# Splitting every large load between the SP and the ACT queue in a decode attention and gated MLP kernel

## The chip, the core and the metric

The kernel runs on one NeuronCore of a Trainium2 chip. TensorE (PE) does the matmuls and transposes, VectorE (DVE) and ScalarE (ACT) the elementwise work, GpSimd (POOL) builds a few masks, and SyncE (SP) issues transfers. A transfer is spread over the core's 16 DMA engines. The metric is the device time of one execution in microseconds (us): 198.85 us, median of 3 runs (198.69 to 199.15).

## The reference

Two blocks work on the same four token vectors, and a sigmoid gate mixes them:

```
g = sigmoid((x * gate_w).sum(-1))                       # x: 4 tokens x 512
q = x @ wq                                              # 32 heads of 128
k, v = last 4096 positions of the caches, 8 kv heads    # 4 batches
a = softmax(q k^T / sqrt(128)) v  @ wo
b = (relu(x @ W_gate) * (x @ W_up)) @ W_down            # 512 -> 1792 -> 512
return g * a + (1 - g) * b
```

All tensors are bf16. Keys and values of the window are 32 MB each, `wq` and `wo` 4 MB each, and the three MLP weights 1.75 MB each. Nothing that is read is used for more than four tokens, so 81 MB come in for little arithmetic.

## The kernel before

The work is cut into eight sets (`NSET`): one batch and four of its kv heads each, that is one 4 MB load of K and one of V (`load_k`, L157, `load_v`, L161). Each of the 128 partitions takes 16,384 columns (32 KB) of a load. `Ksb` and `Vsb` have two buffers each, used in turn. `Wbig` holds `wq` first and `wo` later; the MLP weights go into the K and V buffers when sets 6 and 7 leave them free (L172 to L178).

A small class, `Program`, keeps a list of instructions for each engine, in the order in which the code adds them. `P.op` adds an instruction and `P.dma` a transfer, each with a name that others may wait for. A transfer has its own semaphore, which is complete at 16. The waits stand in front of the instruction on its engine, so whatever an engine has in its list behind a waiting instruction waits too. All large loads are issued by SP, which has nothing else to do: `WQ`, `K0`, `K1`, `V0`, `K2`, `V1` and so on to `K7`, `V6`, then `WG`, `WU` (gate and up), `V7`, `WD` (down) and four pieces `WO 0..3` of `wo` (16, 10, 4 and 2 of its 32 rows of 512 columns, `WO_CUTS`). `K s` waits for the last scores of set s-2, event `("SC", s-2, 3)`; `V s` for the last values matmul of set s-2, `("PV", s-2, 3)`. ACT issues two small loads at the start, `X` (4 KB) and `GW` (1 KB).

One stage s runs the scores of set s beside the softmax and the values of set s-1. The order on each engine is written out by hand (L403 to L432). In a stage PE transposes K in 16 fills of four 128x128 blocks (`kt`, L261), ACT and DVE copy them back over K (L266 for the nine fills in `ACT_TAKES`, L268 for the rest), PE forms scores in four banks (L282), DVE adds a mask and takes maxima (L290), ACT takes exponents in two pieces (L319), DVE transposes them (L326), and PE multiplies with V (`values`, L338). `combine` (L351 to L361) sums the partial results of a set and scales them. The end of a stage on PE is: values piece 1, fill 15, values piece 2, scores bank 3 (which gives `SC s 3`), values piece 3 (which gives `PV s-1 3`). After it DVE finds the maximum (`maximum`, L294) and PE starts fill 0 of the next stage, which waits for `K s+1`; the first copy after it, of fill 0, is ACT's.

After stage 7 come the last exponents, `combine(6)`, the gate and up matmuls (`gateup`, L386), the last values, `combine(7)`, the down matmuls (L446) and the `wo` matmuls (L454), which take the four pieces in order, then one copy (L458) and the store (L459).

Of the kernel before, what the change touches and what calls it, by code (L numbers as in the profile page):

```python
# [13 lines left out]
HQ = 32  # L14
# [5 lines left out]
NSET = 8  # L20
# [59 lines left out]
def bass_gated_mix__sliding_block_cached__glu_gated_reglu__decode_kernel(  # L80
# [13 lines left out]
    with ExitStack() as ctx:  # L94
# [58 lines left out]
        def heads(cache, s):  # L153
            b, half = s // 2, s % 2
            return cache[b, 4 * half:4 * half + 4, SK - WIN:SK, :].rearrange("h (r c) d -> r h (c d)", r=32)

        def load_k(s):  # L157
            P.dma("sp", lambda e: e.dma_start(Ksb[:, s % 2, :], heads(A_k_cache, s)), ("K", s),
                  [("SC", s - 2, NBANK - 1)] if s >= 2 else [])

        def load_v(s):  # L161
            P.dma("sp", lambda e: e.dma_start(Vsb[:, s % 2, :], heads(A_v_cache, s)), ("V", s),
                  [("PV", s - 2, 3)] if s >= 2 else [])

        P.dma("act", lambda e: e.dma_start(xsb[0:4, :], A_x.rearrange("b o d -> (b o) d")), ("X",))
        P.dma("act", lambda e: e.dma_start(xsb[4:5, :], gate_w.rearrange("(o d) -> o d", o=1)), ("GW",))
        P.dma("sp", lambda e: e.dma_start(Wbig[:, :], A_wq.rearrange("(p t) w -> p (t w)", p=128)), ("WQ",))  # L167
        load_k(0)
        for s in range(1, NSET):
            load_k(s)  # L170
            load_v(s - 1)
        P.dma("sp", lambda e: e.dma_start(Ksb[:, 0, 0:4 * FF], B_W_gate.rearrange("(p t) f -> p (t f)", p=128)),  # L172
              ("WG",), [("SC", NSET - 2, NBANK - 1)])
        P.dma("sp", lambda e: e.dma_start(Ksb[:, 0, 4 * FF:8 * FF], B_W_up.rearrange("(p t) f -> p (t f)", p=128)),
              ("WU",), [("SC", NSET - 2, NBANK - 1)])
        load_v(NSET - 1)
        P.dma("sp", lambda e: e.dma_start(Vsb[:, 0, 0:NFT * 512], B_W_down.rearrange("(p i) w -> p (i w)", p=128)),  # L177
              ("WD",), [("PV", NSET - 2, 3)])  # L178
        wo_src = A_wo.rearrange("(p i) w -> p (i w)", p=128)
        for k in range(len(WO_CUTS) - 1):  # L180
            lo, hi = 512 * WO_CUTS[k], 512 * WO_CUTS[k + 1]
            P.dma("sp", lambda e, lo=lo, hi=hi: e.dma_start(Wbig[:, lo:hi], wo_src[:, lo:hi]), ("WO", k), [("Q",)])  # L182


        P.op("pool", lambda e: e.memset(ones[:, :], 1.0), ("ONES",))
# [64 lines left out]
        def kt(s, i):  # L250
            f = len(fills)
            fills.append((s, i))
            tr_of[(s, i)] = f
            bk = trb(f)
            kw = Ksb[:, s % 2, :].bitcast(FP32)
            for cc in range(4):
                c = 4 * i + cc
                w = []
                if cc == 0:
                    w = [("K", s), ("IDENTF",)] + ([copy_done(f - NTR)] if f >= NTR else [])  # L260
                P.op("pe", lambda e, bk=bk, cc=cc, c=c, s=s: e.transpose(  # L261
                    bk[:, cc * 128:(cc + 1) * 128], kw[:, c * 128:(c + 1) * 128], identf[:, :]),
                    ("KT", s, i) if cc == 3 else None, w)
            dst = Ksb[:, s % 2, i * 1024:(i + 1) * 1024]
            if i in ACT_TAKES:
                P.op("act", lambda e: e.activation(dst, bk[:, :].bitcast(BF16), ACTF.Copy), ("KTC", s, i), [("KT", s, i)])  # L266
            else:
                P.op("dve", lambda e: e.tensor_copy(dst, bk[:, :].bitcast(BF16)), ("KTC", s, i), [("KT", s, i)])  # L268
# [60 lines left out]
        def values(s, k):  # L329
            par = s % 2  # L330
            v3 = Vsb[:, par, :].rearrange("p (c w) -> p c w", w=256)
            for c in range(16):
                g = c % 4
                w = []
                if c == 0:
                    w = [("PTT", s, k * NPIECE // 4), ("V", s), ("OSB", s - 1) if s >= 1 else None]
                col = (16 * k + c) * 32
                P.op("pe", lambda e, c=c, g=g, col=col: e.matmul(  # L338
                    OB[32 * g:32 * g + 32, 0:256], pT[:, par, col:col + 32], v3[:, 16 * k + c, :],
                    start=(k == 0 and c < 4), stop=(k == 3 and c >= 12), tile_position=(0, 32 * g)),  # L340
                    ("PV", s, k) if c == 15 else None, w)
            if k == 3:
                P.op("dve", lambda e: e.tensor_copy(osb[:, par, :], OB[:, 0:256]), ("OSB", s),  # L343
                     [("PV", s, 3), ("SUMS", s - 2) if s >= 2 else None])
# [18 lines left out]
        def qproj():  # L363
            for h in range(HQ):
                for t in range(4):
                    P.op("pe", lambda e, h=h, t=t: e.matmul(  # L366
                        FB[:, 64 + 4 * h:68 + 4 * h], Wq3[:, t, 128 * h:128 * h + 128], xT[:, t * 8:t * 8 + 4],
                        start=(t == 0), stop=(t == 3)),
                        ("Q",) if (h == HQ - 1 and t == 3) else None, [("WQ",), ("XTC",), ("G",)])
            P.op("dve", lambda e: e.tensor_copy(qTb[:, :].rearrange("p (b h) -> p b h", b=4),  # L370
                                                FB[:, 64:192].rearrange("p (h b) -> p b h", b=4)), ("QB",), [("Q",)])
            for h in range(2):
                P.op("pe", lambda e, h=h: e.matmul(OB[:, 128 * h:128 * h + 128], perm[:, h, :], qTb[:, :], start=True, stop=True),
                     ("QP",) if h == 1 else None, [("QB",), ("PERM", 1)])
            for g in range(2):
                r = slice(64 * g, 64 * g + 64)
                P.op("dve", lambda e, g=g, r=r: e.tensor_copy(
                    QS[r, :, 16 * g:16 * g + 16], OB[r, 0:256].rearrange("p (s j) -> p s j", j=16)),
                    ("QC", g), [("QP",), ("QZ",)])

        def gateup():
            for i in range(NFT):
                for which, W, key in ((0, Wg, "WG"), (1, Wu, "WU")):
                    col = 64 + 64 * which + 4 * i
                    for t in range(4):
                        P.op("pe", lambda e, W=W, i=i, t=t, col=col: e.matmul(  # L386
                            FB[:, col:col + 4], W[:, t, i:i + NFT * 127 + 1:NFT], xT[:, t * 8:t * 8 + 4],
                            start=(t == 0), stop=(t == 3)),
                            ("GU",) if (i == NFT - 1 and which == 1 and t == 3) else None, [("WG",), ("WU",), ("OQ", NSET - 2)])
            P.op("dve", lambda e: e.tensor_scalar(gtmp[:, :], FB[:, 64:64 + NFT * 4], 0.0, None, op0=ALU.max), ("H0",), [("GU",)])  # L390
            P.op("dve", lambda e: e.tensor_tensor(gtmp2[:, :], FB[:, 128:128 + NFT * 4], gtmp[:, :], ALU.mult), ("H1",), [("H0",)])
            P.op("dve", lambda e: e.tensor_tensor(  # L392
                hT[:, :, :].rearrange("p i (b o) -> p i b o", o=8)[:, :, :, 0], gtmp2[:, :].rearrange("p (i b) -> p i b", b=4),
                gsb[:, 4:8].rearrange("p (o b) -> p o b", o=1).to_broadcast([128, NFT, 4]), ALU.mult), ("H",),
                [("H1",), ("G",), ("HZ",)])
# [4 lines left out]
            kt(0, i)  # L400
        for m in range(NBANK):
            scores(0, m)
        for s in range(1, NSET):  # L403
            maximum(s - 1)
            kt(s, 0)
# [24 lines left out]
            values(s - 1, 2)  # L430
            scores(s, 3)
            values(s - 1, 3)  # L432
        maximum(NSET - 1)
        for k in range(NPIECE):
            exponent(NSET - 1, k)
# [8 lines left out]
        for i in range(NFT):  # L444
            for cb in range(4):
                P.op("pe", lambda e, i=i, cb=cb: e.matmul(  # L446
                    AB[32 * cb:32 * cb + 32, 0:128], hT[:, i, :], Wd[:, i, cb * 128:(cb + 1) * 128],
                    start=(i == 0), stop=False, tile_position=(0, 32 * cb)), None,
                    [("WD",), ("H",), ("SCC", NSET - 1, NBANK - 1)])
        for k in range(len(WO_CUTS) - 1):  # L450
            for i in range(WO_CUTS[k], WO_CUTS[k + 1]):
                for cb in range(4):
                    last = i == 31 and cb == 3
                    P.op("pe", lambda e, i=i, cb=cb: e.matmul(  # L454
                        AB[32 * cb:32 * cb + 32, 0:128], oq[:, i, :], Wo3[:, i, cb * 128:(cb + 1) * 128],
                        start=False, stop=(i == 31), tile_position=(0, 32 * cb)),
                        ("ACC",) if last else None, [("WO", k), ("OQ", NSET - 1)])
        P.op("dve", lambda e: e.tensor_copy(outs[:, :], AB[:, 0:128]), ("OUTS",), [("ACC",)])  # L458
        P.dma("sp", lambda e: e.dma_start(out.rearrange("b o (c d) -> c (b o) d", d=128), outs[0:128:8, :]), ("OUT",), [("OUTS",)])  # L459
        P.op("sp", None, None, [("OUT",)])  # L460
# [50 lines left out]
```

## Time and profile before

| | |
|---|---|
| Time, median of 3 runs | 198.85 us |
| The profiled execution's own time | 198.96 us |
| Its span | 197.1 us |
| Bytes moved | 81.27 MB, 412 GB/s over the span |
| PE, DVE, ACT busy | 71%, 52%, 46% of the span |
| K loads, issue to landing (median) | 23.3 us |
| V loads, issue to landing (median) | 32.4 us |
| Last `wo` piece, issue to landing | 23.8 us |

The span is the time from the first to the last record of the profiled execution; 1.9 us of its time lie outside it. The profile page also cuts the span in 40 slices and gives for each the busy share of every engine and of the 16 DMA engines. The chain that ended last follows the last instruction back through what released each step. The trace also keeps a record of every DMA packet (its queue, start, length and bytes); a packet here is one partition's run of a load, 32 KB for a K or V load.

### The profile page before, as it was taken

What the parts mean: (1) busy time and instruction counts of PE and PEld (TensorE: products, weight loads), DVE (VectorE), ACT (ScalarE), POOL (GpSimd) and SP (SyncE); (2) the same over time, 40 slices, a digit from 0 to 9 for tenths busy, and PEclk for the clock granted to TensorE, in tenths of its full rate; (3) what the DMA queues carried; (4) which work ended last, traced back from release to release, by engine and by line L of the source; (5) the groups of instructions that cost most, each with busy time, mean ns of one, the idle gap of its engine ahead of it and who ended that gap; (6) DMA issues with size and microseconds to landing.
All of it is one profiled execution on the core that took longest, in us unless ns stands there. A gap on an engine that the chain in (4) does not pass through costs nothing.

```text
span 197.1 us, 4202 instructions
## 1 busy us (share of the span) xinstructions
PE 140.5 (71%) x1858; PEld 107.1 (54%) x1858; DVE 103.4 (52%) x278; ACT 91.6 (46%) x108; POOL 6.1 (3%) x31
## 2 busy tenths in 40 slices
PE   0134099869789829994998399839991999497734
PEld 0033087536466428753865386438751875397533
DVE  2102044998589446855694388437845595741200
ACT  2000069698298309760983288319740876220000
POOL 7400000000000000000000000000000000000000
PEclk9999999999999975998899979966997599965855
DMA  6999999999999999999999999999999999999980
GB/s 220 426 445 452 435 445 439 422 426 421 429 426 426 422 426 432 424 439 429 445 432 435 432 426 417 432 439 429 432 426 422 432 399 425 449 435 406 421 340 32
DMA packets 3503, 81.27 MB, mean 412 GB/s; under 512 B 409, under 2 KB 414, under 8 KB 670
## 3 DMA queue, kind: packets, MB, share of 16 engines
q1 hardware_dynamic: 3476, 81.01, 96.2%
q8 instruction: 14, 0.23, 0.5%
q14 instruction: 3, 0.02, 0.0%
q10 hardware_dynamic: 10, 0.01, 0.0%
HBM read 81.01 MB, written 0.00 MB: 411 GB/s over the span
## 4 chain that ended last, share of the span: by engine, by line
DMA 58%; PE 29%; ACT 9%; DVE 2%; issue 1%; SPq 1%
DMA Ksb<-in_A_k_cache_dram 46%; PE bank L261 18%; DMA Wbig<-in_A_wo_dram 12%; ACT Ksb L266 7%; PE bank L282 5%; PE bank L338 2%; PE bank L351 2%; DVE Ksb L268 1%; ACT sc L319 1%; PE bank L454 1%; ACT L319 1%; SPq L182 0%; SPq L167 0%; SPq L177 0%; DVE outs L458 0%
## 5 line engine op out<-in xcount | busy, mean ns | idle before, releaser
L261 PE MATMUL bank<-identf,Ksb 128*128 128x128 f32 x512 | 81.0, 312 | 31.0 <-DMA Ksb<-in_A_k_cache_dram 26.5
L266 ACT ACTIVATE Ksb<-bank 128x1024 bf16<-128x1024 bf16 x72 | 70.9, 1022 | 69.2 <-PE bank L261 68.8
L261 PEld LDWEIGHTS bank<-identf,Ksb 128*128 128x128 f32 x512 | 66.1, 160 | 46.0 <-DMA Ksb<-in_A_k_cache_dram 28.4
L268 DVE COPY Ksb<-bank 128x1024 bf16<-128x1024 bf16 x56 | 38.0, 685 | 43.0 <-PE bank L261 42.0
L290 DVE CUSTOM_DVE_ANT_0 sc<-bank,mask 128x512 bf16<-128x512 f32 x32 | 21.7, 684 | 9.5 <-PE bank L282 9.4
L338 PE MATMUL bank<-Vsb,pT 128*32 128x256 bf16 x512 | 20.8, 291 | 1.0 <-DVE hT L392 1.0
L282 PE MATMUL bank<-Ksb,QS 128*32 128x512 bf16 x256 | 19.4, 384 | 2.1 <-DVE Ksb L268 1.6
L326 DVE STREAM_TRANSPOSE pT<-sc 128x1024 bf16<-128x1024 bf16 x16 | 19.7, 1236 | 1.7 <-ACT sc L319 1.5
L319 ACT ACTIVATE sc<-sc,negmax 128x1024 bf16<-128x1024 bf16 x16 | 18.3, 1146 | 4.8 <-DVE negmax L311 4.7
L338 PEld LDWEIGHTS bank<-Vsb,pT 128*32 128x32 bf16 x512 | 13.2, 101 | 7.2 <-issue 2.4
L351 PEld LDWEIGHTS bank<-osb,Wsel 128*64 128x64 f32 x128 | 8.1, 138 | 4.6 <-issue 2.6
L351 PE MATMUL bank<-osb,Wsel 128*64 128x32 f32 x128 | 8.9, 224 | 1.2 <-DVE mq L297 0.7
L282 PEld LDWEIGHTS bank<-Ksb,QS 128*32 128x32 bf16 x256 | 4.1, 94 | 9.3 <-DVE Ksb L268 3.9
L386 PE MATMUL bank<-xT,Ksb 128*128 128x4 bf16 x112 | 6.9, 199 | 1.8 <-DVE oq L359 1.8
L386 PEld LDWEIGHTS bank<-xT,Ksb 128*128 128x128 bf16 x112 | 6.8, 163 | 1.9 <-issue 1.9
L454 PE MATMUL bank<-Wbig,oq 128*32 128x128 bf16 x128 | 4.2, 311 | 4.0 <-DMA Wbig<-in_A_wo_dram 4.0
L366 PE MATMUL bank<-xT,Wbig 128*128 128x4 bf16 x128 | 3.6, 166 | 3.7 <-DMA Wbig<-in_A_wq_dram 3.7
L228 PE MATMUL bank<-ident,xsb 5*128 5x5 bf16 x4 | 0.3, 166 | 8.2 <-DMA xsb<-in_gate_w_dram 8.2
L454 PEld LDWEIGHTS bank<-Wbig,oq 128*32 128x32 bf16 x128 | 3.1, 139 | 5.0 <-DMA Wbig<-in_A_wo_dram 5.0
L366 PEld LDWEIGHTS bank<-xT,Wbig 128*128 128x128 bf16 x128 | 3.5, 104 | 3.7 <-DMA Wbig<-in_A_wq_dram 3.7
L343 DVE COPY osb<-bank 128x256 f32<-128x256 f32 x8 | 3.4, 420 | 3.8 <-PE bank L338 3.8
L311 DVE TENSOR_SCALAR negmax<-mall 32x1 f32<-32x1 f32 x32 | 4.6, 144 | 1.0
(54 smaller groups left out, 42.4 us busy)
## 6 DMA issues: line engine op xcount, KB each, us to landing
Ksb<-in_A_k_cache_dram SPq DMA_DIRECT2D x8, 4096.0 KB, 23.3
Vsb<-in_A_v_cache_dram SPq DMA_DIRECT2D x8, 4096.0 KB, 32.4
Wbig<-in_A_wq_dram SPq DMA_DIRECT2D x1, 4096.0 KB, 12.2
Wbig<-in_A_wo_dram SPq DMA_DIRECT2D x1, 2048.0 KB, 20.3
Ksb<-in_B_W_gate_dram SPq DMA_DIRECT2D x1, 1792.0 KB, 18.5
Ksb<-in_B_W_up_dram SPq DMA_DIRECT2D x1, 1792.0 KB, 22.5
Vsb<-in_B_W_down_dram SPq DMA_DIRECT2D x1, 1792.0 KB, 15.8
Wbig<-in_A_wo_dram SPq DMA_DIRECT2D x1, 1280.0 KB, 22.9
```

Source lines behind the costliest of these rows:

```text
L261: P.op("pe", lambda e, bk=bk, cc=cc, c=c, s=s: e.transpose(bk[:, cc * 128:(cc + 1) * 128], kw[:, c * 128:(c + 1) * 128], identf[:, :]), (" ...
L266: P.op("act", lambda e: e.activation(dst, bk[:, :].bitcast(BF16), ACTF.Copy), ("KTC", s, i), [("KT", s, i)])
L268: P.op("dve", lambda e: e.tensor_copy(dst, bk[:, :].bitcast(BF16)), ("KTC", s, i), [("KT", s, i)])
L282: P.op("pe", lambda e, a=a, h=h: e.matmul(bk[32 * a:32 * a + 32, 0:512], QS[:, NSET * h + s, :], k4[:, 16 * bank:16 * bank + 16, 32 * a:32 ...
L290: P.op("dve", lambda e: e.tensor_tensor_reduce(sc[:, s % 2, bank * 512:(bank + 1) * 512], bk[:, :], mask[:, :], 1.0, LOWEST, ALU.add, ALU.max,
L319: P.op("act", lambda e: e.activation(sc[:, par, k * PW:(k + 1) * PW], sc[:, par, k * PW:(k + 1) * PW], ACTF.Exp, bias=negmax[:, par:par + ...
L326: P.op("dve", lambda e: e.transpose(pT[:, par, k * PW:(k + 1) * PW], sc[:, par, k * PW:(k + 1) * PW]), ("PTT", s, k), [("EXP", s, k), ("PV ...
L338: P.op("pe", lambda e, c=c, g=g, col=col: e.matmul(OB[32 * g:32 * g + 32, 0:256], pT[:, par, col:col + 32], v3[:, 16 * k + c, :], start=(k ...
L351: P.op("pe", lambda e, k=k, lo=lo: e.matmul(FB[r, 256:288], Wsel[:, lo:lo + 64], osb[:, par, 32 * k:32 * k + 32], start=(k == 0), stop=(k ...
L366: P.op("pe", lambda e, h=h, t=t: e.matmul(FB[:, 64 + 4 * h:68 + 4 * h], Wq3[:, t, 128 * h:128 * h + 128], xT[:, t * 8:t * 8 + 4], start=(t ...
L386: P.op("pe", lambda e, W=W, i=i, t=t, col=col: e.matmul(FB[:, col:col + 4], W[:, t, i:i + NFT * 127 + 1:NFT], xT[:, t * 8:t * 8 + 4], star ...
L454: P.op("pe", lambda e, i=i, cb=cb: e.matmul(AB[32 * cb:32 * cb + 32, 0:128], oq[:, i, :], Wo3[:, i, cb * 128:(cb + 1) * 128], start=False, ...
```

## The change

Every large load is made of two halves by columns. A helper, `both`, issues the first half on SP and the second on ACT, each with a semaphore of its own, and whoever waited for a load waits for both halves. As ACT's instructions run in the order of its list, its loads can't all stand ahead of its other work: only `WQ`, `K0`, `K1` and `V0` do, and the later ones are added at the end of stage s by `loads_after(s)`, for both queues, in the old order.

```diff
+        def both(name, dst, src, n, waits=()):
+            for j, q in enumerate(("sp", "act")):
+                lo, hi = j * n // 2, (j + 1) * n // 2
+                P.dma(q, lambda e, lo=lo, hi=hi: e.dma_start(dst[:, lo:hi], src[..., lo:hi]), name + (q,), waits)
+
         def load_k(s):
-            P.dma("sp", lambda e: e.dma_start(Ksb[:, s % 2, :], heads(A_k_cache, s)), ("K", s),
-                  [("SC", s - 2, NBANK - 1)] if s >= 2 else [])
+            both(("K", s), Ksb[:, s % 2, :], heads(A_k_cache, s), 16384, [("SC", s - 2, NBANK - 1)] if s >= 2 else [])
...
-        P.dma("sp", lambda e: e.dma_start(Wbig[:, :], A_wq.rearrange("(p t) w -> p (t w)", p=128)), ("WQ",))
+        both(("WQ",), Wbig[:, :], A_wq.rearrange("(p t) w -> p (t w)", p=128), 16384)
         load_k(0)
-        for s in range(1, NSET):
-            load_k(s)
-            load_v(s - 1)
...
+        load_k(1)
+        load_v(0)
...
+        def loads_after(s):
+            if s + 2 < NSET:
+                load_k(s + 2)
+            if s + 2 == NSET:
+                free = [("SC", s, NBANK - 1)]
+                both(("WG",), Ksb[:, 0, 0:4 * FF], B_W_gate.rearrange("(p t) f -> p (t f)", p=128), 4 * FF, free)
+                both(("WU",), Ksb[:, 0, 4 * FF:8 * FF], B_W_up.rearrange("(p t) f -> p (t f)", p=128), 4 * FF, free)
+            if s + 1 < NSET:
+                load_v(s + 1)
+            else:
+                both(("WD",), Vsb[:, 0, 0:NFT * 512], B_W_down.rearrange("(p i) w -> p (i w)", p=128), NFT * 512, [("PV", NSET - 2, 3)])
+                for k in range(len(WO_CUTS) - 1):
+                    lo, hi = 512 * WO_CUTS[k], 512 * WO_CUTS[k + 1]
+                    both(("WO", k), Wbig[:, lo:hi], wo_src[:, lo:hi], hi - lo, [("Q",)])
...
-                    w = [("K", s), ("IDENTF",)] + ([copy_done(f - NTR)] if f >= NTR else [])
+                    w = [("K", s, "sp"), ("K", s, "act"), ("IDENTF",)] + ([copy_done(f - NTR)] if f >= NTR else [])
...
         for m in range(NBANK):
             scores(0, m)
+        loads_after(0)
         for s in range(1, NSET):
...
             values(s - 1, 3)
+            loads_after(s)
```

The other places that waited for a load (`values`, `qproj`, `gateup`, the down and the `wo` matmuls) wait for both halves in the same way.

## The prediction

> **What bounds the kernel now.** I read the slices first, then the queues, the chain, the waits, and the windows of the end.
>
> The slices and the queues of the page:
>
> ```profile
> DMA  6999999999999999999999999999999999999980
> GB/s 220 426 445 452 435 445 439 422 426 421 429 426 426 422 426 432 424 439 429 445 432 435 432 426 417 432 439 429 432 426 422 432 399 425 449 435 406 421 340 32
> q1 hardware_dynamic: 3476, 81.01, 96.2%
> q8 instruction: 14, 0.23, 0.5%
> PE 140.5 (71%) x1858; PEld 107.1 (54%) x1858; DVE 103.4 (52%) x278; ACT 91.6 (46%) x108; POOL 6.1 (3%) x31
> ```
>
> The 16 DMA engines are 90% busy or more in every slice but the first and the last two, at 399 to 452 GB/s. One queue, q1, which is SP's, fills them alone: it never lacks work. No compute engine is above 71%. The chain in order of time says the same; each K load in it is the end of a backlog, with a stage of compute behind it:
>
> ```profile
> 1.24 23.00 DMA Ksb<-in_A_k_cache_dram
> ...
> 52.13 20.69 DMA Ksb<-in_A_k_cache_dram
> ...
> 89.21 22.42 DMA Ksb<-in_A_k_cache_dram
> ...
> 127.13 24.90 DMA Ksb<-in_A_k_cache_dram
> ...
> 169.42 22.89 DMA Wbig<-in_A_wo_dram
> ```
>
> A K load alone needs 4.19 MB / 430 GB/s = 9.8 us; the rest of its 20 to 25 us is what stood ahead of it. So K could be issued later at no loss, as long as the backlog lasts. PE's waits and SP's waits:
>
> ```profile
> PE bank L261 <- DMA Ksb<-in_A_k_cache_dram: 26.5, 7, 6.9
> PE bank L454 <- DMA Wbig<-in_A_wo_dram: 4.0, 2, 2.9
> ACT sc L319 <- DVE negmax L311: 4.7, 1, 4.7
> ```
>
> PE waits for K seven times (K0, K2 to K7), for K0 6.9 us and for the others (26.5 - 6.9)/6 = 3.3 us on average, and at the end for `wo`. The windows of the end (columns after the five engines: clock, DMA share, GB/s):
>
> ```profile
> 189.00:190.00 1.00, 0.72 (x28) 0.72 (x32) 0.00 (x0) 0.00 (x0) 0.00 (x0) 0.50 1.04 428
> 190.00:191.00 1.00, 1.00 (x47) 0.91 (x36) 0.00 (x0) 0.00 (x0) 0.00 (x0) 0.50 0.77 311
> 191.00:192.00 1.00, 0.18 (x8) 0.00 (x0) 0.00 (x0) 0.00 (x0) 0.00 (x0) 0.50 0.51 205
> 192.00:193.00 1.00, 0.65 (x28) 0.65 (x32) 0.00 (x0) 0.00 (x0) 0.00 (x0) 0.50 0.45 168
> 193.00:194.00 1.00, 1.00 (x40) 0.69 (x32) 0.00 (x0) 0.00 (x0) 0.00 (x0) 0.50 0.15 55
> ```
>
> The DMA engines end one after another between 190.4 and 193.8 us (packet records): each has the same bytes, but those that also fetched instructions (q8) fall behind. The last one sets the end: 193.8, then the last matmuls, copy and store.
>
> So the time is the slowest DMA engine's: its packets one after another. What the change does to the packets decides; what it does to the compute decides only if a queue runs dry or the compute of the end falls behind `wo`.
>
> **Part 1, twice as many packets, half as long.** In the packet records a 32 KB packet lasts 1213 ns (median of 2,176: 1214) and the next starts 3 ns before its end, so one costs 1210. The other sizes that occur last 613 ns (16 KB, `wo` piece 0), 538 (14 KB), 387 (10 KB), 159 (4 KB), 84 (2 KB), 44 to 46 (1 KB) and 9 (the 4 bytes of a semaphore), less the same 3. Two of 16 KB cost 1220, 10 ns more than one of 32 KB: a fixed cost of some 10 ns per packet. Each engine has 8 packets and one semaphore per load. Per 4 MB load: 8 x 10 + 6 = 0.086 us; from landings instead, the quickest engine took 9.70 us per 4 MB load and 4.90 for the 2 MB `wo` piece, so 2 x 4.90 - 9.70 = 0.10. For 17 loads 1.46 to 1.7 us: I take 1.6. Gate, up and down: a 7 KB packet, between the 4 and the 10 KB rows, would cost 270, two of them 5 more than the 535 of 14 KB: 3 x (8 x 5 + 6 ns) = 0.14. The `wo` pieces, in the same way 6, 4, 6 and 3 ns a pair: 8 x 19 + 4 x 6 ns = 0.18. Together +1.9 us on every engine.
>
> Is that cost still paid when the two queues alternate? No row of before has two queues busy for long; the nearest is `GW`, on ACT's queue amid SP's `WQ`. Its 1 KB packet ran alone, 17,595 to 17,641 ns on the trace's clock (6.48 us in the span), between two 32 KB packets of 1213 ns each that were neither longer nor shorter; its semaphore came exactly one SP packet later and took its 9 ns. So engines take one packet of each queue in turn, a change of queue costs nothing, and nothing is hidden under the other queue: I take +1.9. The other bound: the second queue hides every fixed cost. Before pays it on 192 packets and 24 semaphores per engine, 192 x 10 + 24 x 6 ns = 2.1 us, so -2.1 us. The far row upward is an instruction fetch on q8: 16 KB lasted 1004 ns and made the next SP packet 1681 instead of 1213; at 0.47 us for each of 384 packets that would be 180 us, but `GW`, data on its way to the same memory, showed none of it, so I leave it out of the range.
>
> The Trainium skill, "DMA: Bandwidth & Descriptors", section "Rules for kernel authors", speaks against the change: spreading DMAs over the issuing engines gains no bandwidth, since all run on the same 16 DMA engines and interleave, and it saves issue time only. By that rule alone the sum would be 198.9, no change; the `GW` row agrees with the interleaving, and the packet lengths add the 1.9.
>
> **Part 2, the order of arrival.** Issue: SP's `WQ` goes at 0.81; ACT issues `X` (0.80, 0.56 us) and `GW` (1.39, 0.23 us) first, so its half goes at about 1.65. `GW`, issued at 1.39, was served only after four 32 KB packets of SP on its engine. So SP's half will be ahead by 4 packets of 16 KB (if the engine takes four packets in advance) to 8 (if it takes 128 KB): 2.4 to 4.9 us, and engine 0 one or two packets more. A load has landed when ACT's half has, so `WQ` and K0 land later by that much; I take 3.7. `WQ` is needed before K0 only (PE waits for K0 6.9 us), K0 starts stage 0, and stage 0's end issues K2: 36.48 becomes about 40.2. The backlog then ends with V0, on the first engine at 41.23 (records), with part 1 at about 41.6. The first packet of `WQ` came 1.0 us after its issue, so K2's come at 41.2: just in time. Cost taken 0; with the lead of 4.9 plus two packets (1.2) it is 36.48 + 6.1 + 1.0 - 41.6 = 2.0 us of idle DMA: upper end. Below zero is excluded, for this queue was never empty before. At K2 the lead shrinks to what ACT still has of V0. Later K issues have more backlog (K5: issued 89.21, V3 ahead of it ends at 99.6 or later), so 3 us of delay there cost nothing.
>
> **Part 3, ACT's own time.** At the end of each stage ACT waits for `SC s 3` and `PV s-1 3` and issues K and V: by SP's rows 0.53 + 0.60 us. Behind the waits in its list stands only the copy of fill 0, which needs a transpose that PE runs after both, so the waits delay nobody. The 1.1 us of issue lie under PE's wait for K (3.3 us on average). Only in stage 1, where K1 is there, does the copy start 1.1 - 0.6 = 0.5 us late, and that goes into K2's wait. After stage 7 ACT issues `WD` and four `wo` halves, 0.33 + 1.86 = 2.2 us, within its 4.7 us wait for negmax. Cost 0. Without these covers it would be 7 x 1.1 + 2.2 = 10 us. SP keeps its order and drops nothing; PE's extra semaphore waits fall where it waits anyway: 0.
>
> **Part 4, the end.** If ACT's queue is behind, its share of `wo` pieces 1 to 3 comes last and alone. PE took 1.90 us for the 64 matmuls of piece 0, and pieces 1 to 3 are 64 more. Before, piece 1 landed 2.3 us ahead of PE's last matmul. With only ACT's halves of pieces 2 and 3 behind it (24 KB per engine, 0.9 us, plus packet costs 0.1) PE would end 1.9 us after piece 1, 0.9 after the last landing instead of 0.5: 0 to 0.4, I take 0.2. K7 may land up to 4 us later against the end before compute decides: PE idles 2.9 + 1.2 + 0.4 us among the `wo` matmuls.
>
> **Sum.** +1.9 + 0 + 0 + 0.2 = 2.1 on the profiled execution's 198.96 (197.1 span and 1.9 around it) gives 201.1; that execution lies 0.1 above the median of 198.85, so 201.0.
>
> **Rivals.** (a) Faster: the fixed packet cost is hidden. One packet's end overlaps the start of another queue's. For it: packets of one queue already overlap by 3 ns. Against: `GW`. -2.1 + 0.2 gives 197.0; it decides as soon as more than half of the cost per packet vanishes. (b) No change: half of it is hidden, so +0 and the end +0.2: 198.6 to 199.2. (c) Slower still: the DMA runs dry before K2, because the lead of SP's half delays K0 beyond 3.7 us plus what I took: up to +2.0, so 201.5 to 203.0. For it: `GW`'s long wait; against: margin 0.4 us even at a lead of 3.7. (d) The two queues don't have work at once, because ACT is stuck behind compute: then ACT's halves land last and alone; the bytes and packets are the same, PE's wait for K grows, and the time stays near 201, up to 203 if `wo`'s half is late.
>
> **How the numbers follow.** What a measurement can tell is about 0.2% (0.4 us). My forecast (200.0 to 201.8) has 0.54; (a) 0.18; (b) 0.08; (c) and (d) together 0.20. So faster 0.18, same 0.08, slower 0.74. The range leaves out 0.1 on each side: 197.6 to 203.0; the forecast's own is 200.0 to 201.8.
>
> **What would show it.** Right: about 3,070 data packets of 32 KB and less become 6,140, 16 KB packets cost 610 ns each in turn (or last 1220 where two are counted at once), the DMA share stays at 9 through slice 36, the last `wo` piece lands near 195.8, K0 lands 2 to 5 us later, ACT's waits for L261 shrink by its issues, and K2's first packets follow V0's at once. Wrong: packet pairs that cost less than 1210 (a) or much more than 1220; a slice of DMA below 9 near 41 us (c); PE's waits among the `wo` matmuls gone, with compute as the end; ACT's DMA issues much longer than SP's 0.6 us.

## The result and the profile after

The changed kernel takes 200.86 us (median of 4 runs, 200.80 to 201.02) against 198.98 us before: a ratio of 1.0097, with a 95% interval of 1.0080 to 1.0115. The forecast was 201.0. Here and below, times and ratios leave out the few executions that took over 1.5% longer than the fastest of the same kernel. The profiled execution took 200.85 us, against 198.96 before, with a span of 199.0 us against 197.1.

The slices and the queues of the page of the changed kernel (in the slices, each entry is a fortieth of the span; in the queues, packets, MB and the share of the 16 engines' time):

```profile
span 199.0 us, 4246 instructions
DMA  6999999999999999999999999999999999999980
GB/s 218 432 438 438 418 425 428 431 425 435 426 415 425 435 425 423 431 428 418 428 431 428 425 435 423 418 421 428 435 428 421 423 412 431 430 418 412 415 328 29
DMA packets 6959, 81.27 MB, mean 408 GB/s; under 512 B 793, under 2 KB 1054, under 8 KB 2334
q1 hardware_dynamic: 3476, 40.51, 48.4%
q10 hardware_dynamic: 3466, 40.51, 48.2%
```

The bytes are now shared evenly by two queues, and the number of packets has doubled. The DMA engines were full before and are full now. The two queues together hold the engines for 96.6% of the span, where one held them for 96.2%: the second queue found no idle time to fill. The same bytes go at 408 GB/s in place of 412.

The K loads and the last `wo` load in the chain that ended last, in order of time (start, us):

```profile
2.08 24.65 DMA Ksb<-in_A_k_cache_dram
...
57.15 17.25 DMA Ksb<-in_A_k_cache_dram
...
89.65 23.92 DMA Ksb<-in_A_k_cache_dram
...
130.33 23.86 DMA Ksb<-in_A_k_cache_dram
...
171.20 22.87 DMA Wbig<-in_A_wo_dram
```

It is the same chain as before. K3 is issued 5 us later (57.15 for 52.13), yet `wo` is issued only 1.8 us later: the delay of the first stages is absorbed by the backlog. The waits that answer to those shown of before (us in total, times, longest):

```profile
PE bank L268 <- DMA Ksb<-in_A_k_cache_dram: 21.1, 6, 6.1
PE bank L463 <- DMA Wbig<-in_A_wo_dram: 2.5, 2, 1.3
ACT sc L326 <- DVE negmax L318: 4.7, 1, 4.7
```

PE waits for K 5.4 us less, and this is no gain: what PE lost in the first stages it no longer waits for later. By the packet records the last byte of the inputs lands at 195.41 us, against 193.77: +1.64. From there to the last copy (L467) it is 1.17 us against 0.92: +0.25. The sum, 1.89, is the whole difference of the two profiled executions.

### The profile page after: what moved, and what is told of

Read it like the earlier page. It is cut to its first block, busy times and chain, and to the rows that moved or that the text cites. A ratio compares the mean times of both kernels' runs of the same rounds, so it can differ in the third digit from the quotient of the medians.

```text
span 199.0 us, 4246 instructions
## 1 busy us (share of the span) xinstructions
PE 143.2 (72%) x1858; PEld 108.5 (55%) x1858; DVE 103.9 (52%) x278; ACT 91.4 (46%) x108; POOL 6.3 (3%) x31
## 2 busy tenths in 40 slices
DMA packets 6959, 81.27 MB, mean 408 GB/s; under 512 B 793, under 2 KB 1054, under 8 KB 2334
## 4 chain that ended last, share of the span: by engine, by line
DMA 57%; PE 21%; ACT 10%; DVE 8%; ACTq 2%; issue 1%
DMA Ksb<-in_A_k_cache_dram 45%; PE bank L268 13%; DMA Wbig<-in_A_wo_dram 11%; ACT Ksb L273 7%; PE bank L289 4%; DVE Ksb L275 3%; DVE pT L333 3%; ACT sc L326 2%; PE bank L345 2%; ACTq L160 2%; DVE sc L297 1%; PE bank L463 1%; ACT L326 1%; PE bank L358 1%; DVE oq L366 0%
## 5 line engine op out<-in xcount | busy, mean ns | idle before, releaser
L289 PE MATMUL bank<-Ksb,QS 128*32 128x512 bf16 x256 | 20.5, 403 | 2.0 <-DVE Ksb L275 1.6
L358 PEld LDWEIGHTS bank<-osb,Wsel 128*64 128x64 f32 x128 | 8.8, 148 | 5.2 <-issue 3.2
L358 PE MATMUL bank<-osb,Wsel 128*64 128x32 f32 x128 | 9.7, 233 | 1.2 <-DVE mq L304 0.7
```

Of the source, the lines that this page charges most:

```text
L289: P.op("pe", lambda e, a=a, h=h: e.matmul(bk[32 * a:32 * a + 32, 0:512], QS[:, NSET * h + s, :], k4[:, 16 * bank:16 * bank + 16, 32 * a:32 ...
L358: P.op("pe", lambda e, k=k, lo=lo: e.matmul(FB[r, 256:288], Wsel[:, lo:lo + 64], osb[:, par, 32 * k:32 * k + 32], start=(k == 0), stop=(k ...
```

## The experiments

All are edits of the changed kernel. The packet theory says that a packet has a fixed cost, whatever its queue, and that cutting the loads is the whole loss. The rival, the queue theory, says that two queues lose by taking turns, or by the order of arrival that this gives.

**1. The same halves, all on SP.**

```diff
-                P.dma(q, lambda e, lo=lo, hi=hi: e.dma_start(dst[:, lo:hi], src[..., lo:hi]), name + (q,), waits)
+                P.dma("sp", lambda e, lo=lo, hi=hi: e.dma_start(dst[:, lo:hi], src[..., lo:hi]), name + (q,), waits)
```

> All loads cut into the same halves, all issued by SP, none by ACT beyond the two small ones. Packet theory (a DMA packet has a fixed cost of 8 to 10 ns, whatever its queue): the same 6,144 data packets and as many semaphores as in the changed kernel, so the last byte lands at 195.2 to 195.6 us, as there (195.4), and the time is 200.6 to 200.9. Queue theory (the loss comes from two queues taking turns, or from the order of arrival that they give): one queue again, so the last byte at 193.8 and the time at 199.0, as before. K0 starts the transposes at 24.5 us by both (26.9 in the changed kernel).

Measured: 200.56 us, ratio 1.0085 (1.0070 to 1.0100); last byte at 195.38. The page of this run:

```profile
DMA packets 6959, 81.27 MB, mean 409 GB/s; under 512 B 793, under 2 KB 1054, under 8 KB 2334
q1 hardware_dynamic: 6932, 81.01, 96.6%
q10 hardware_dynamic: 10, 0.01, 0.0%
```

One queue alone carries the 6,932 packets, K0's transposes begin at 24.37 us as before, ACT issues nothing large, and nearly the whole loss is there. So it came from the cut, not from the second queue. The landings let the cost be read load by load. On the mean of the 16 engines `wq` has landed 0.08 us earlier than before and K7, 14 loads later, 0.98 us later: 1.06 / 14 = 0.076 us per load, that is 8 more packets and one more semaphore. With 6 ns for the semaphore, 8.7 ns per packet.

**2. Quarters, all on SP.**

```diff
-            for j, q in enumerate(("sp", "act")):
-                lo, hi = j * n // 2, (j + 1) * n // 2
-                P.dma(q, lambda e, lo=lo, hi=hi: e.dma_start(dst[:, lo:hi], src[..., lo:hi]), name + (q,), waits)
+            for j, q in enumerate(("a", "sp", "b", "act")):
+                lo, hi = j * n // 4, (j + 1) * n // 4
+                P.dma("sp", lambda e, lo=lo, hi=hi: e.dma_start(dst[:, lo:hi], src[..., lo:hi]), name + (q,), waits)
```

Whoever waited for two halves waits for four quarters.

> Four quarters per load, all on SP. Packet theory: 768 data packets and 96 semaphores per engine in place of 192 and 24, so 576 x 8 to 10 ns + 72 x 6 ns = 5.0 to 6.2 us above before, and a few tenths for four waits in a row at the end: 204.0 to 205.6 us. Queue theory: 199.0. If the two halves of a load cost something else that doesn't grow with the packets (one more load in the queue, one more wait), it is three times the 1.9 us of the changed kernel only by chance.

Measured: 203.78 us, ratio 1.0246 (1.0229 to 1.0263), a little under what was expected; last byte at 198.60, 4.83 us later than before. In the same reading of the landings `wq` is 0.17 us earlier and K7 3.03 us later: 3.20 / 14 = 0.229 us per load, with 24 more packets and three more semaphores, (0.229 - 0.018) / 24 = 8.8 ns per packet. The cost per packet is the same as for halves, and the loss of the last byte is three times theirs (4.83 against 1.61 to 1.64), as it should be for three times the extra packets. Quarters also mean three times as many extra transfers, so this run alone can't tell a cost per packet from a cost per transfer; experiment 4 can.

**3. Halves by partitions, on two queues, packets of full length.**

```diff
+            rows = src.shape[0] // 2
             for j, q in enumerate(("sp", "act")):
-                lo, hi = j * n // 2, (j + 1) * n // 2
-                P.dma(q, lambda e, lo=lo, hi=hi: e.dma_start(dst[:, lo:hi], src[..., lo:hi]), name + (q,), waits)
+                P.dma(q, lambda e, j=j: e.dma_start(dst[64 * j:64 * j + 64, :], src[rows * j:rows * j + rows]),
+                      name + (q,), waits)
```

> Both queues have work at once, but the halves are cut by partitions (64 each), so that a packet stays as long as before: 3,072 data packets, twice the semaphores. Packet theory: only 24 more semaphores per engine at 6 ns, so the last byte lands at 193.8 to 194.1, and the time is 199.0 to 199.5, some 0.25 of it for the second wait at the end. Queue theory: two queues take turns as in the changed kernel, time 200.7 to 201.0. [...]

Measured: 358.03 us, ratio 1.80. Both theories missed. Packets of 32 KB last 2253 ns (median), where they lasted 1214. To see whether the two queues have a part in it, the same halves were issued by SP alone (`P.dma("sp", ...)`):

> The halves by partition (0 to 63, 64 to 127) of the 358 us run, all on SP. If the 358 us come from which engine writes which partitions, all 16 engines now write one half of the partitions at a time, and it is as slow or slower: 355 to 375 us, packets of 32 KB near 2.4 us. If they come from the two queues, 199.0 to 199.5.

Measured: 378.30 us (one execution), packets of 32 KB 2474 ns; its 81.27 MB in a span of 376.6 us are 216 GB/s. The queues on the page of the run on two queues:

```profile
DMA packets 3887, 81.27 MB, mean 228 GB/s; under 512 B 793, under 2 KB 798, under 8 KB 1054
q1 hardware_dynamic: 1940, 40.51, 48.6%
q10 hardware_dynamic: 1930, 40.51, 48.2%
```

There are as few packets as with whole loads, at little more than half the rate. With one queue it is slower still, so the queues are not the cause; what the two runs share is that a transfer reaches only 64 neighbouring partitions. The Trainium skill, "SBUF — State Buffer", section "Door 1: The DMA port swizzle", says that partitions 0 to 63 reach only 8 of the 16 ports through which DMA writes, and gives some 218 GB/s for them; the 216 GB/s of the run on SP agree. With both halves under way at once, on two queues, it is 228, and no run here shows why that is not more. As a test of the second queue this cut was useless, so another one was needed.

**4. Halves by even and odd partitions, on two queues, packets of full length.**

```diff
             for j, q in enumerate(("sp", "act")):
-                lo, hi = j * n // 2, (j + 1) * n // 2
-                P.dma(q, lambda e, lo=lo, hi=hi: e.dma_start(dst[:, lo:hi], src[..., lo:hi]), name + (q,), waits)
+                part = src[:, j:4:2, :] if len(src.shape) == 3 else src[j:128:2, :]
+                P.dma(q, lambda e, j=j, part=part: e.dma_start(dst[j:128:2, :], part), name + (q,), waits)
```

> [...] 3,072 data packets of up to 32 KB, twice the semaphores. Packet theory: 24 semaphores per engine x 6 ns and some 0.2 us at the end: last byte at 193.7 to 194.1, time 199.0 to 199.5. Queue theory: 200.6 or more. If the 358 us of the halves by partition came from the second queue, or from transfers of 64 partitions as such, this one is as slow.

Measured: 201.20 us, ratio 1.0121 (1.0106 to 1.0136): a miss, and on the side of the queue theory. But the packets are not longer (1213 ns), and the loss is not spread over the run. The windows between 40 and 44 us, first of the changed kernel, then of this one (after the five engines: clock, DMA share, GB/s):

```profile
40.00:41.00 1.00, 1.00 (x10) 0.77 (x8) 0.93 (x6) 0.00 (x0) 0.00 (x0) 1.00 0.87 360
41.00:42.00 1.00, 0.01 (x1) 0.00 (x0) 0.83 (x6) 0.00 (x0) 0.00 (x0) 1.00 1.09 426
42.00:43.00 1.00, 0.00 (x0) 0.00 (x0) 0.82 (x6) 0.91 (x1) 0.00 (x0) 1.00 1.03 442
43.00:44.00 1.00, 0.66 (x4) 0.42 (x4) 0.83 (x2) 1.00 (x2) 0.00 (x0) 1.00 0.88 377
```

```profile
40.00:41.00 1.00, 0.93 (x9) 0.69 (x7) 0.93 (x6) 0.00 (x0) 0.00 (x0) 1.00 1.21 508
41.00:42.00 1.00, 0.00 (x0) 0.00 (x0) 0.81 (x5) 0.00 (x0) 0.00 (x0) 1.00 0.56 197
42.00:43.00 1.00, 0.00 (x0) 0.00 (x0) 0.84 (x6) 0.94 (x2) 0.00 (x0) 1.00 0.91 262
43.00:44.00 1.00, 0.65 (x4) 0.42 (x4) 0.80 (x2) 1.00 (x2) 0.00 (x0) 1.00 0.81 262
```

(A packet counts in a window by its start, so single windows can pass the full rate.) Here the DMA ran partly dry: by the packet records only 7 or 8 of the 16 engines were at work between 41.8 and 42.2 us, as V0 was through there before K2's packets came. K2 was issued no later than in the changed kernel (39.52 against 39.60), and its first packets came 2.1 us after that, against 1.8; why they were later, no run shows. Outside of this gap the rate was that of before: on the mean of the engines SP's halves of V1 and V6 landed 97.80 us apart, ten loads, against 97.87 for those loads before. This is the third rival of the prediction, in a kernel that was not the predicted one. A first attempt to close the gap, with ACT's half of `wq` moved ahead of `x` and `gate_w`:

> The halves by even and odd partitions again, with 3,072 packets of full length on two queues, but ACT issues its half of wq ahead of x and gate_w. In the run without that the DMA stood partly idle between 41 and 45 us, where K2 came after the end of V0, and the last byte landed at 196.0. If that idle time was its whole loss, K0 now begins about 1.5 us earlier, K2 is issued at 38.5 or before, no slice at 40 to 50 us is below 410 GB/s, the last byte lands at 193.7 to 194.3 and the time is 199.0 to 199.6. If two queues lose by taking turns, the idle time goes and 200.5 or more stays.

Measured: 200.74 us, 200.29 to 201.43, ratio 1.0089 (1.0074 to 1.0103), last byte at 196.09. The expectation failed at its first step: `x` and `gate_w` now came so late that PE first worked at 18.4 us; K2 was issued at 40.31, later than before the edit, and the 40 to 45 us slice fell to 371 GB/s. The gap stayed, so this run tells nothing of the theories. The second attempt left the first four loads whole and on SP:

```diff
+            if name in (("WQ",), ("K", 0), ("K", 1), ("V", 0)):
+                P.dma("sp", lambda e: e.dma_start(dst, src), name + ("sp",), waits)
+                P.events[name + ("act",)] = P.events[name + ("sp",)]
+                return
```

> The first four loads (wq, K0, K1, V0) whole and on SP, as in the kernel before; from K2 on halves by even and odd partitions on both queues, with packets of full length. In the two earlier runs of this kind the loads from K2 to V6 took 9.78 us each on the mean of the engines, as before (9.79), and what was lost was lost at the start and where K2 came too late. Here K2 is issued at 36.5 as before, so that gap can't open. Packet theory: 20 semaphores per engine x 6 ns and 0.1 to 0.25 us at the end: last byte 193.7 to 194.2, time 199.0 to 199.5. If two queues lose by taking turns: 200.3 or more. V0 has to share with K2's half on ACT and may land near 47 us, just before the first values matmuls (48 us), which must not become a gap.

Measured: 199.04 us, ratio 1.0002 (0.9993 to 1.0011); last byte at 193.84, 0.07 later than before. The queues of this run:

```profile
DMA packets 3823, 81.27 MB, mean 412 GB/s; under 512 B 729, under 2 KB 734, under 8 KB 990
q1 hardware_dynamic: 2196, 48.90, 58.1%
q10 hardware_dynamic: 1610, 32.12, 38.1%
```

Two queues with work at once, from K2 to the last piece of `wo`, cost nothing and gain nothing as long as the packets stay whole; what is left is within about 0.1%. Twenty of the 24 loads are two transfers here, so a transfer more costs next to nothing either: the loss of the halves and quarters goes by packets. The queue theory is out.

**5. Whole loads in turn on the two queues**, nothing cut: K1 to K7 on SP, K0 and V0 to V6 on ACT, `wq` and what comes last in turn:

```diff
+        turns = [0]
+
         def both(name, dst, src, n, waits=()):
-            for j, q in enumerate(("sp", "act")):
-                lo, hi = j * n // 2, (j + 1) * n // 2
-                P.dma(q, lambda e, lo=lo, hi=hi: e.dma_start(dst[:, lo:hi], src[..., lo:hi]), name + (q,), waits)
+            q = ("sp", "act")[turns[0] % 2]
+            turns[0] += 1
+            P.dma(q, lambda e: e.dma_start(dst[:, 0:n], src), name + ("sp",), waits)
+            P.events[name + ("act",)] = P.events[name + ("sp",)]
```

> Both queues have work at once, but no load is cut: they take whole loads in turn, so K goes to SP and V to ACT (and the later weights in turn). Packets and semaphores as in the kernel before. Packet theory: the last byte at 193.6 to 194.0. But K and V now share the engines, so K7 lands up to 7 us later than the 152 us of before, and the compute behind it (34 us to the scaled values of set 7, 4 us of wo matmuls) may end at 194 to 198 in place of 194.7: time 199.0 to 202. Queue theory: the last byte at 195.4 or later.

Measured: 203.62 us (203.06 to 205.59), ratio 1.0264 (1.0204 to 1.0324); last byte at 197.27, not 193.6 to 194.0. The slices of its page:

```profile
GB/s 255 443 443 417 423 413 443 449 433 417 431 413 391 430 420 436 436 430 433 404 348 425 430 426 391 430 422 430 391 420 423 423 315 437 456 417 414 417 355 19
```

The packets are as before (32 KB: 1213 ns), but five slices fall to between 315 and 391 GB/s; each slice is 5.03 us, and against 425 GB/s the five miss 3.4 us, which is what the last byte is late. The DMA ran partly dry in them: its share falls to 0.67 between 61 and 62 us, after loads issued at 58.80, and to 0.79 between 100 and 101 us, after loads issued at 99.17. The likely reason is that K and V share the engines, so K lands later, its stage ends later and the next loads are issued later; no run took that apart. It fits the parity runs: the order of arrival costs nothing only while the backlog lasts.

**6. ACT's half of `wq` ahead of its two small loads**, in the changed kernel:

```diff
+        both(("WQ",), Wbig[:, :], A_wq.rearrange("(p t) w -> p (t w)", p=128), 16384)
         P.dma("act", lambda e: e.dma_start(xsb[0:4, :], A_x.rearrange("b o d -> (b o) d")), ("X",))
         P.dma("act", lambda e: e.dma_start(xsb[4:5, :], gate_w.rearrange("(o d) -> o d", o=1)), ("GW",))
-        both(("WQ",), Wbig[:, :], A_wq.rearrange("(p t) w -> p (t w)", p=128), 16384)
```

> The changed kernel, but ACT issues its half of wq before the two small loads x and gate_w, so its half goes at 0.8 us as SP's does, and SP has no lead. Transposes of K0 begin at 24.5 to 25.3 us in place of 26.9. If the order of arrival costs nothing, as the DMA stays full, the last byte and the time stay where they were: 195.2 to 195.6 and 200.6 to 201.0. If the late K0 was part of the loss, 199.5 to 200.3.

Measured: 200.92 us, ratio 1.0104 (1.0087 to 1.0121); last byte at 195.60. K0's transposes began at 25.48 (expected 24.5 to 25.3), 1.4 us earlier than in the changed kernel, and the end did not move: the late K0 was no part of the loss.

**7. One semaphore for both halves**, one wait for 32 (`P.dma` can now be given a semaphore):

```diff
...
-                P.dma(q, lambda e, lo=lo, hi=hi: e.dma_start(dst[:, lo:hi], src[..., lo:hi]), name + (q,), waits)
+                P.dma(q, lambda e, lo=lo, hi=hi: e.dma_start(dst[:, lo:hi], src[..., lo:hi]), name + (q,), waits,
+                      None if j == 0 else P.events[name + ("sp",)][0])
+            for q in ("sp", "act"):
+                P.events[name + (q,)] = (P.events[name + (q,)][0], 32)
```

> The changed kernel, but both halves of a load count on one semaphore, and whoever waits does so once, for 32. In the changed kernel PE's last wo matmuls begin 0.71 us after the last byte, in the kernel before 0.45. If the second wait in a row costs this: 0.45 to 0.5 here, and a time of 200.6. If it is the lag of ACT's queue, or the landing itself: still 0.7, and 200.9. The last byte at 195.4 by both.

Measured: 200.60 us, ratio 1.0090 (1.0075 to 1.0105), not to be told from the changed kernel's 1.0097 by its interval. In the profiled execution, at 200.98 us the longest of the four, the last byte is at 195.69 (expected 195.4). The last `wo` matmuls begin 0.64 us after the last byte, not 0.45 to 0.5: the expectation failed, and the chains say why. The chain at the end, first before, then after, then with one semaphore (start, us; "issue" is time without a wait that the profile shows):

```profile
192.30 0.04 issue
192.35 1.87 PE bank L454 x43
194.21 0.02 issue
194.23 0.43 PE bank L454 x8
```

```profile
194.07 0.14 issue
194.21 1.26 PE bank L463 x40
195.47 0.01 issue
195.47 0.62 PE bank L463 x16
196.09 0.04 issue
196.13 0.43 PE bank L463 x7
```

```profile
194.34 0.04 issue
194.38 1.26 PE bank L467 x40
195.64 0.04 issue
195.69 0.62 PE bank L467 x16
196.31 0.03 issue
196.33 0.43 PE bank L467 x8
```

In all three, PE works without a pause from the landing of `wo` piece 1 to the end, 2.3 us. So the end hangs on piece 1, not on the last byte. Piece 1 landed 1.46 us ahead of the last byte before (192.31 against 193.77) and 1.34 us ahead after (194.07 against 195.41): 0.12 us. The second wait is the 0.10 us by which "issue" grew from 0.04 to 0.14, and one semaphore brings that back to 0.04. Together 0.22 of the 0.25 us.

No kernel here beats the one before beyond its interval. What the runs leave of the time is the bytes over a DMA that is full from the second slice to the last but two.

## Why the prediction was right

**What bounds the kernel.** Right: the DMA is full in both profiles, and the time went up by the last byte's 1.64 us plus 0.25 at the end.

**Part 1, packets.** Right in cause, a little too large: 1.9 was taken, 1.64 measured. The data packets went from 3,072 to 6,144, and one of 16 KB lasts 613 ns, on either queue. The term that was mis-sized is the 1.6 us for the 17 large loads, 0.094 each: the row of the landings that pulled it up (0.10) was too high, and the run on SP alone shows 0.076, that is 1.29 us. Against it stands a small gain at the start (0.08) that was not foreseen. With the 0.14 and 0.18 of the other weights this gives 1.53, against 1.61 on SP alone and 1.64 in the changed kernel.

**Nothing is hidden under the other queue.** Right, and now shown: rivals (a) and (b) would have needed packets that cost less when the queues alternate. One queue with the same packets lost as much (experiment 1), and two queues with whole packets lost nothing (the last of experiment 4). The rule that the prediction cites from the Trainium skill ("DMA: Bandwidth & Descriptors", section "Rules for kernel authors"), that spreading DMAs over the issuing engines adds no bandwidth, agrees with both.

**Part 2, the order of arrival.** The cost of zero was right, the way to it partly luck. The lead was worked out from a misread row: ahead of `GW` on its engine stood three 32 KB packets of SP, not four (SP's first packets begin at 1.82 us and last up to 2.3 us, the two behind them 1.21 each, and `GW` comes at 6.48). ACT's first large packet started at 5.61 us, when SP had started 82, that is 5 per engine: the forecast was 4 to 8. K0's transposes began 2.6 us later (forecast 3.7), K2 was issued at 39.60 (forecast 40.2). But K2's first packets came 1.8 us after their issue, at 41.4, and not 1.0 us; so they did come "just in time", by two errors that cancelled. That rival (c) was a real one is seen in experiment 4: there K2, issued at nearly the same time, came too late.

**Part 3, ACT's own time.** The cost of zero was right, one figure was not. The issues of K2 and V1 on ACT in the changed kernel:

```profile
39.60 0.58 ACTq L160 DMA_DIRECT2D Ksb<-in_A_k_cache_dram  x1
40.22 1.82 ACTq L160 DMA_DIRECT2D Vsb<-in_A_v_cache_dram  x1
42.09 1.94 ACT L273 ACTIVATE Ksb<-bank 128x1024 bf16<-128x1024 bf16 x2 [3.57 <-issue]
```

SP's rows had said 0.53 and 0.60; V1's took 1.82 us, so the first copy of stage 1 began 1.9 us after the transposes that it waits for (40.15), in place of 0.5. The prediction had named issues much longer than 0.6 us on ACT as a sign of being wrong; this one was, and still cost nothing. It went where the prediction put it, into PE's wait for K. At the end the five issues (170.32 to 172.62) lay within ACT's wait for negmax, as forecast.

**Part 4, the end.** 0.2 forecast, 0.25 measured. The mechanism given, piece 1 of `wo` moving closer to the last byte, makes 0.12 of it; the second wait, which the prediction had put at 0, makes 0.10.

**Sum.** 2.1 forecast, 1.89 measured: 0.26 too much in part 1, 0.05 too little at the end.

## What to carry to other kernels

With the DMA engines full, a second issuing queue added nothing here; look at the share of the DMA engines, not at how many queues have work. What a change does to the number of packets can be priced from the packet lengths of the trace, here 10 ns by the forecast and 8.7 as measured for each extra packet on each engine, and that alone foretold most of the loss. If a load must be cut, cut it so that the runs stay long and each part reaches partitions all over the memory: even and odd partitions cost nothing here from K2 on (cut from the first load on, they cost 1.2% through one gap), the lower and the upper half cost 80%.

## What the runs showed of the hardware

- Transfers that reach only 64 neighbouring partitions went at 216 to 228 GB/s on all 16 DMA engines, half the rate of transfers over 128, or over every second partition (experiments 3 and 4).
- Issuing can wait by itself. Four `wo` pieces took SP 1.86 us to issue in the kernel before; their eight halves took 10.44 us when all loads were halves on SP, with many halves still outstanding there, and the sixteen quarters 19.84 us. The DMA stayed full and SP had nothing else to do; no run tried it on ACT, which has copies and exponents behind its issues.
- From issue to the first packet it took 1.0 us for the first load of the program, 1.8 us for SP's half of K2 in the changed kernel, and 4.3 us for ACT's half of K2 in the last run of experiment 4 (36.90 to 41.18 us), where ACT's queue was empty and SP's was not.
- An instruction fetch of 16 KB set one DMA engine back by 1.4 us in the kernel before: of the 16 engines that loaded K0 before, 15 were done between 21.87 and 22.40 us and the one with a fetch at 23.82. These setbacks spread the engines' ends over some 3 us (190.4 to 193.8 us), and the slowest engine sets the end.
